# A fused linear-attention and gated-FFN kernel: the first k block turned as fp32, and one new order for all operations

## The chip, the cores and the metric

The kernel runs on one core of a Trainium2 chip. The core has five engines with a queue each: TensorE (PE: matmuls, with weight loads shown as PEld), VectorE (DVE), ScalarE (ACT), GpSimd (POOL) and SyncE (SP, which here only issues DMAs). Each takes its instructions in program order and waits on semaphores for what the others make. The metric is the device time of one execution in microseconds (us); lower is better.

## What is computed

Attention with exponential feature maps over q, k and v of shape [8, 8, 576, 64] (batch, head, token, head dimension), then a feed-forward block with a gate over the 4608 tokens of width 512:

```python
def phi(x):
    proj = np.einsum('bhsd,df->bhsf', x, w_phi)             # w_phi: 64 x 128
    proj = proj - np.max(np.abs(proj), axis=-1, keepdims=True)
    return np.concatenate([np.exp(proj), np.exp(-proj)], axis=-1)
q_p, k_p = phi(q), phi(k)
kv  = np.einsum('bhsf,bhsd->bhfd', k_p, v)
z   = np.sum(k_p, axis=2)
num = np.einsum('bhsf,bhfd->bhsd', q_p, kv)
den = np.einsum('bhsf,bhf->bhs', q_p, z)[..., None] + 1e-06
x   = (num / den).transpose(0, 2, 1, 3).reshape(4608, 512)
gate = np.maximum(x @ w_gate, 0.0)                          # w_gate, w_val: 512 x 1536
out  = gate * (x @ w_val) @ w_out                           # w_out: 1536 x 512
```

## The kernel before

All matmuls are bf16 with fp32 accumulation in eight PSUM banks. A batch is 512 tokens in four chunks of 128 (`C` = 4) and 64 left over; the left-over tokens of pairs of batches make a ninth group. The heads are taken in three groups, 0 to 1, 2 to 4 and 5 to 7 (`HEADS`).

The order of everything is written out by hand as data: `ORDER` is a string of some 2,000 words, one for each operation, such as `ke.0.1.2.0:4@kp0`. The name before the first dot picks the function `do_ke`, the numbers are its arguments, the digits behind the colon are its PSUM banks, and what stands behind `@` is the buffer that a tile takes in its ring. The last lines of the kernel run through the words and call the functions, so that each engine's queue is the words of that engine in the order of the string. A word that comes later in the string can still run earlier in time if it is on another engine and waits for nothing.

The words that the texts below speak of, for batch `b`, head group `j`, chunk `i`:

- Loads. `lf` (L445, SP) brings k of batch 0, heads 2 to 4, as fp32 into the storage of `xTm`; `lk` (POOL) brings other k with a cast to bf16, `lm` and `lq` small pieces of k and q in the same way, `lv` and `lw` bring v, `wl` a third of w_val (0) or w_gate (1), `wo` a third of w_out, `ln` the left-over q. `wr` (L393, on ACT's queue) and `wq` (the same on SP's) load w_phi twice over into 128 partitions, `wd` (L402) casts it, `w1` and `wa` make the second layout of it.
- First k. `cf` and `cg` (L453) cast what `lf` brought, on DVE and ACT. `k0` (L584) turns six blocks of 128 x 128 on PE as bf16 matmuls with the identity, `k1` (L587) copies the result to `kT`, `k2` (L605) multiplies with w_phi: twelve matmuls into four banks, one for each chunk. Later batches turn k on DVE (`kt`, `ku`) and multiply in `kr`.
- Features of k. `ke` (L614, ACT) is the exponential of plus or minus the projection, `kx` (L622, DVE) the largest absolute value, `kk` and `kp` (L631, L642, ACT) its exponential. `vs`, `vq`, `vo` (POOL) and `vd`, `vp` (DVE) scale v by it. `kv` (L718, PE) sums over the tokens, `kc` (L729, ACT) copies the sums.
- Features of q. `q0` and `q1` turn q, `qb` (L764, PE) projects it, `qe` (L793, ACT) and `qx` (L801, DVE) as for k; `qy`, `qz`, `qu` and `qw` spread the largest value over the partitions (`qy` on PE at L811 with an fp32 identity, `qz` the DVE maximum `my` at L819).
- Division. `nu` (L841, PE) multiplies q's features with the sums, `nt`, `nv` and `nr` (L862, L872, L880, DVE) add the two signs and invert, `nx` (L884, POOL) normalizes to `xu`.
- Feed-forward. Batch 0 turns `xu` on PE (`xp` at L906, copied by `xa` on ACT), then works by chunk: `pv` and `pg` (L1029), 16 matmuls of 128 columns each. Otherwise `fv` and `fg` (L1000) make value and gate with four matmuls of 512 columns, `ga` (L1021) multiplies them, `fo` (L1061) is the second matmul, `od` stores.
- `zz.n` (L425) is n matmuls of 256 columns of zeros into a bank that nobody reads: filler for PE.

Batch 0's attention has to be through its first chunk before the feed-forward can start; from then on feed-forward matmuls of one batch are mixed with the attention of the next.

Of the kernel before, what the change touches and what calls it, by code (L numbers as in the profile page):

```python
# [8 lines left out]
FP32 = mybir.dt.float32  # L9
# [7 lines left out]
ms.0 ms.4@vr0 wr ms.3@vr1 lf id sl ms.5 ms.6 ms.2 lw.0.1 lw.0.0 if cf.1 lk.0.2 lk.0.0 wd cg.0  # L17
zz.18:0 k0.1:0 k1.1:0@kT0 lm.0.1 lm.0.0 zz.1:1 w1:2 lq.0.1 lq.0.0 wa:2 zz.2:1 k2.1:0345
ke.0.1.2.0:4@kp0 lv.0.2 kx.0.1.1:3@mk0 lv.0.1 ke.0.1.3.1:5 kx.0.1.2:4 zz.2:1 k0.2:2 k1.2:2@kT1
ke.0.1.1.0:3 ke.0.1.2.1:4 kx.0.1.0:0 kx.0.1.3:5 ke.0.1.1.1:3 zz.7:1 k2.2:2674 ke.0.2.0.1:2@kp1  # L20
ke.0.2.2.0:7 kx.0.2.1:6@mk1 ke.0.2.0.0:2 ke.0.1.0.0:0 k0.0:3 k1.0:3@kT1 wl.0.0 ke.0.1.3.0:5
kx.0.2.2:7 kx.0.2.0:2 lv.0.0 zz.6:1 q0.1:3 q1.1:3@qT0 ke.0.2.1.1:6 ke.0.2.2.1:7 kx.0.2.3:4 zz.1:1
q0.0:5 q1.0:5@qT1 ke.0.2.1.0:6 zz.4:1 k2.0:2736 lm.1.1 lk.1.3 lm.1.0 kx.0.0.0:2@mk2 ke.0.1.0.1:0
kx.0.0.2:3 ke.0.2.3.0:4 kx.0.0.1:7 kp.0.2.1:4 kk.0.1.0@ek0 lq.1.2 kk.0.1.1 qb.1.0:0 qe.0.1.0.1:0@qp0
vo.1@vs0 kp.0.2.0:4 kx.0.0.3:6 vp.2:4@vs1 vs.0.1.0 qb.1.1:5 qe.0.1.1.0:5@qp1 qe.0.1.0.0:0 qx.0.1.1:5
ke.0.0.1.0:7@kp2 qx.0.1.0:0 vd.0.2.0:4 vs.0.1.1 kk.0.0.0@ek1 ke.0.0.3.0:6 zz.18:1 qb.0.1:0
ke.0.0.2.1:3 ke.0.0.1.1:7 qx.0.0.1:0 qb.0.2:7 qx.0.0.2:7 ke.0.2.3.1:4 wl.0.1 kk.0.0.1 vq.0.1
ke.0.0.0.1:2 ke.0.0.3.1:6 ke.0.0.0.0:2 zz.6:1 qb.0.0:6 vs.0.0.0@vs2 vq.0.0 qx.0.0.0:6 zz.5:1
# [232 lines left out]
def kernel(  # L261
# [16 lines left out]
    P = 128  # L278
# [615 lines left out]
    def do_ny(bk, b, i):  # L894
        normalize(nc.vector, b, i)
# [257 lines left out]
```

## Time and profile before

| | |
|---|---|
| time, median of 3 runs | 376.44 us (373.83, 376.44, 376.68) |
| profiled execution | 377.31 us, of which the span from first to last instruction is 375.5 us |
| mean granted PE clock over the span | 0.990 |
| bytes read from and written to HBM | 37.81 MB and 9.44 MB |
| matmuls in the span | 3614, 75 of them fillers |

A line of the timeline has the start, the time from the first start to the last end of the instructions that it merges, the engine, the line in the code, the operation, the tiles written and read and their count; brackets tell how long the engine stood idle before it and what ended that. A line of the stages has the stage, its length, and the busy time of PE, weight loads, DVE, ACT and POOL with their counts, then the PE clock that was granted (1.00 is full), the mean number of DMA queues busy as a share, and GB/s. A DMA line has the transfer, its count, its size and the time from issue to landing.

### The profile page before, as it was taken

The numbers are of one execution on the slowest core, as the hardware profiler recorded it, in microseconds if no ns is written. First come the engines' busy times: TensorE is split into PE (matmuls) and PEld (weight loads), VectorE is DVE, ScalarE is ACT, GpSimd is POOL, SyncE is SP. The second block draws the span as 40 slices with busy tenths as digits, with TensorE's granted clock in tenths as the row PEclk, the third lists the DMA queues.
The fourth block names the chain that finished last, engine by engine and source line by source line (L and its number), as shares of the span: only waits on it lengthen the run. The fifth ranks groups of instructions, "written<-read, shape, count | busy, mean of one in ns | idle before, by whom it ended". The sixth has DMA issues, their size and how long they took to land.

```text
span 375.5 us, 9202 instructions
## 1 busy us (share of the span) xinstructions
PE 367.3 (98%) x3614; PEld 196.7 (52%) x3614; DVE 290.4 (77%) x672; ACT 228.5 (61%) x550; POOL 157.3 (42%) x163
## 2 busy tenths in 40 slices
PE   8798999999999999999999999999999999999996
PEld 5567857446544554564455444554444644444444
DVE  5969999998989899999978795888675646534441
ACT  4979996999768873987865556846764301212111
POOL 8774496549349138912770343513045013100000
PEclk9969999999999999999999999999999999999999
DMA  9999998973974992393438052183330022200114
GB/s 141 248 201 199 149 133 119 151 117 58 176 184 71 181 139 70 68 190 76 100 61 152 17 95 66 46 148 51 107 89 17 2 72 82 58 2 15 41 30 141
DMA packets 90381, 38.10 MB, mean 101 GB/s; under 512 B 64226, under 2 KB 85602, under 8 KB 90338
## 3 DMA queue, kind: packets, MB, share of 16 engines
q0 software_dynamic: 33504, 15.03, 31.4%
q1 hardware_dynamic: 56560, 22.29, 26.7%
q8 instruction: 28, 0.46, 0.5%
q10 hardware_dynamic: 274, 0.20, 0.2%
q14 instruction: 15, 0.12, 0.1%
HBM read 37.81 MB, written 9.44 MB: 126 GB/s over the span
## 4 chain that ended last, share of the span: by engine, by line
PE 93%; DVE 2%; DMA 2%; POOL 1%; ACT 1%; issue 0%; POOLq 0%; ACTq 0%
PE bank L1000 47%; PE bank L1061 24%; PE bank L718 6%; PE bank L841 4%; PE bank L1029 4%; PE bank L778 2%; PE bank L562 2%; DMA qn<-in_q_dram 2%; PE bank L982 1%; PE bank L1092 1%; PE bank L764 0%; PE bank L425 0%; POOL kn L434 0%; DVE mk L622 0%; DVE u L872 0%
## 5 line engine op out<-in xcount | busy, mean ns | idle before, releaser
L1061 PE MATMUL bank<-wo,h 128*128 128x512 bf16 x420 | 97.8, 379 | 0.0
L614 ACT ACTIVATE kp<-bank 128x384 bf16<-128x384 f32 x192 | 83.5, 509 | 16.4 <-PE bank L562 11.2
L1015 ACT CAST val<-bank 128x512 bf16<-128x512 f32 x81 | 47.2, 594 | 73.1 <-PE bank L1000 67.5
L1021 DVE SCALAR_TENSOR_TENSOR h<-bank,val 128x512 bf16<-128x512 f32 x100 | 67.1, 681 | 28.9 <-PE bank L1000 14.4
L1000 PE MATMUL bank<-xTs,wv 128*128 128x512 bf16 x352 | 87.1, 379 | 0.0
L1000 PE MATMUL bank<-xTs,wg 128*128 128x512 bf16 x352 | 86.4, 379 | 0.0
L884 POOL TENSOR_TENSOR xu<-u,r 128x512 bf16<-128x512 f32 x36 | 37.2, 1040 | 99.2 <-DVE r L880 72.5
L793 ACT ACTIVATE qp<-bank 128x512 bf16<-128x512 f32 x128 | 70.0, 619 | 10.7 <-PE bank L778 9.0
L1061 PEld LDWEIGHTS <-h 128*128 128x128 bf16 x420 | 39.2, 98 | 45.8 <-issue 2.4
L669 POOL TENSOR_TENSOR vs<-vn,ek 128x780 bf16<-128x780 f32 (+3 forms) x40 | 52.8, 1341 | 24.0 <-ACT ek L631 13.4
L1000 PEld LDWEIGHTS <-wg 128*128 128x128 bf16 x400 | 37.5, 98 | 41.6 <-issue 1.1
L1000 PEld LDWEIGHTS <-wv 128*128 128x128 bf16 x400 | 37.0, 98 | 41.1 <-issue 1.3
L622 DVE TENSOR_REDUCE mk<-bank 128x3 f32<-128x384 f32 x96 | 49.7, 541 | 3.5 <-ACT kp L614 1.4
L801 DVE TRANSPOSE_TENSOR_REDUCE maxq<-bank 128x16 f32<-128x512 f32 x64 | 42.4, 693 | 7.1 <-ACT qp L793 3.2
L872 DVE TENSOR_TENSOR u<-bank,t 128x195 f32<-128x195 f32 (+1 forms) x108 | 33.8, 331 | 2.4 <-POOL xu L884 0.4
L862 DVE TENSOR_TENSOR t<-bank,cq 128x195 f32<-128x195 f32 (+1 forms) x96 | 29.9, 327 | 7.0 <-PE bank L841 6.2
L841 PEld LDWEIGHTS <-qp 128*128 128x128 bf16 x512 | 22.5, 98 | 11.9 <-issue 1.5
L697 POOL TENSOR_TENSOR vr<-vm,ek 64x520 bf16<-64x520 f32 x16 | 16.9, 1055 | 23.4 <-ACT ek L631 15.9
L841 PE MATMUL bank<-kv,qp 128*128 128x65 bf16 x512 | 25.3, 193 | 0.0
L718 PEld LDWEIGHTS <-kp 128*128 128x128 bf16 x640 | 23.0, 101 | 3.9 <-ACT qp L793 1.0
L718 PE MATMUL bank<-vs,kp 128*128 128x65 bf16 x512 | 23.8, 198 | 0.0
L1070 ACT COPY ob<-bank 128x512 f32<-128x512 f32 x19 | 11.3, 595 | 20.4 <-PE bank L1061 19.5
(97 smaller groups left out, 355.2 us busy)
## 6 DMA issues: line engine op xcount, KB each, us to landing
out_dram<-ob SPq DMA_DIRECT2D x31, 256.0 KB, 2.4
vn<-in_v_dram SPq DMA_DIRECT2D x24, 256.0 KB, 4.2
kn<-in_k_dram POOLq DMA_DIRECT2D x7, 512.0 KB, 9.7
qn<-in_q_dram POOLq DMA_DIRECT2D x7, 512.0 KB, 7.6
wv<-in_moe_w_val_dram POOLq DMA_DIRECT2D x3, 512.0 KB, 11.4
wg<-in_moe_w_gate_dram POOLq DMA_DIRECT2D x3, 512.0 KB, 8.6
wo<-in_moe_w_out_dram POOLq DMA_DIRECT2D x3, 512.0 KB, 7.7
out_dram<-ob SPq DMA_DIRECT2D x9, 128.0 KB, 2.3
```

The source lines that it names most:

```text
L614: nc.scalar.activation(kp_of(3 * b + j)[:, i, s].rearrange("p n f -> p (n f)"), bank[bk[0]][:, 0 : 3 * F], AF.Exp, scale=(1.0, -1.0)[s],)
L622: nc.vector.tensor_reduce(mk_of(3 * b + j)[:, :, i], bank[bk[0]][:, 0 : 3 * F].rearrange("p (n f) -> p n f", f=F), axis=AX.X, op=ALU.max, ...
L669: nc.gpsimd.tensor_tensor(vs_of(3 * b + j)[:, s, 0:n].rearrange("p n i e -> p (n i) e")[:, :, 0:e], src[:, lo:hi].rearrange("p h i e -> p ...
L718: nc.tensor.matmul(out_ps[:, h - lo, s, :], lhsT=lhsT, rhs=rhs, start=(at == 0), stop=(at == 2 * n * (C + 1) - 1),)
L793: nc.scalar.activation(qp_of(4 * b + i)[:, s, 4 * hq : 4 * hq + 4].rearrange("p h m -> p (h m)"), bank[bk[0]], AF.Exp, scale=(1.0, -1.0)[s],)
L801: nc.vector.tensor_reduce(maxq[:, :, i, 4 * hq : 4 * hq + 4].rearrange("p t h -> p h t"), bank[bk[0]].rearrange("p (h t u) -> p h t u", h= ...
L841: nc.tensor.matmul(bank[bk[0]][:, E * n : E * (n + 1)], lhsT=qp_of(4 * b + i)[:, s, h, :], rhs=kv_of(b)[:, h, s, 0:E],)
L884: eng.tensor_tensor(xu_of(n).rearrange("p (h d) -> p h d", d=D), u_of(n)[:, :, 0:D], r_of(n).to_broadcast([P, H, D]), op=ALU.mult,)
L1000: nc.tensor.matmul(bank[bk[0]], lhsT=w[:, dc, P * f : P * f + P], rhs=xT(g)[:, dc, :], start=(dc == 0), stop=(dc == NDC - 1),)
L1015: nc.scalar.copy(val_of(NFC * g + f), bank[bk[0]])
L1021: nc.vector.scalar_tensor_tensor(h2_of(g, f), bank[bk[0]], 0.0, val_of(NFC * g + f), op0=ALU.max, op1=ALU.mult)
L1061: nc.tensor.matmul(bank[bk[0]], lhsT=h2_of(g, f)[:, P * t : P * t + P], rhs=wo_sb[:, f, :], start=(f == 0), stop=(f == NFC - 1),)
```

## The change

The order string is replaced as a whole. The words are the same but for these: `wr`, `cf.1`, `cg.0`, `k0.1`, `k1.1`, `k2.0`, `k2.1` and `k2.2` are gone; `wq`, `kf.1`, `kf.0`, `kg.1`, `kh.0` and `k3.j.c` (six of them) are new; and the fillers are 77, placed otherwise. `lf`'s fp32 data is no longer cast: `kf.c` turns it on PE as fp32 with the fp32 identity, three matmuls for each half, and `kg.1` (DVE) and `kh.0` (ACT) copy the two halves to `kT` as bf16. `k3` is `k2` cut in two, two banks each. w_phi is issued by SP behind `lf` instead of by ACT. The last 1,469 words keep their order; banks and buffers are assigned anew everywhere.

Up to the first turned x block the order before was:

```
ms.0 ms.4@vr0 wr ms.3@vr1 lf id sl ms.5 ms.6 ms.2 lw.0.1 lw.0.0 if cf.1 lk.0.2 lk.0.0 wd cg.0
zz.18:0 k0.1:0 k1.1:0@kT0 lm.0.1 lm.0.0 zz.1:1 w1:2 lq.0.1 lq.0.0 wa:2 zz.2:1 k2.1:0345
ke.0.1.2.0:4@kp0 lv.0.2 kx.0.1.1:3@mk0 lv.0.1 ke.0.1.3.1:5 kx.0.1.2:4 zz.2:1 k0.2:2 k1.2:2@kT1
ke.0.1.1.0:3 ke.0.1.2.1:4 kx.0.1.0:0 kx.0.1.3:5 ke.0.1.1.1:3 zz.7:1 k2.2:2674 ke.0.2.0.1:2@kp1
ke.0.2.2.0:7 kx.0.2.1:6@mk1 ke.0.2.0.0:2 ke.0.1.0.0:0 k0.0:3 k1.0:3@kT1 wl.0.0 ke.0.1.3.0:5
kx.0.2.2:7 kx.0.2.0:2 lv.0.0 zz.6:1 q0.1:3 q1.1:3@qT0 ke.0.2.1.1:6 ke.0.2.2.1:7 kx.0.2.3:4 zz.1:1
q0.0:5 q1.0:5@qT1 ke.0.2.1.0:6 zz.4:1 k2.0:2736 lm.1.1 lk.1.3 lm.1.0 kx.0.0.0:2@mk2 ke.0.1.0.1:0
kx.0.0.2:3 ke.0.2.3.0:4 kx.0.0.1:7 kp.0.2.1:4 kk.0.1.0@ek0 lq.1.2 kk.0.1.1 qb.1.0:0 qe.0.1.0.1:0@qp0
vo.1@vs0 kp.0.2.0:4 kx.0.0.3:6 vp.2:4@vs1 vs.0.1.0 qb.1.1:5 qe.0.1.1.0:5@qp1 qe.0.1.0.0:0 qx.0.1.1:5
ke.0.0.1.0:7@kp2 qx.0.1.0:0 vd.0.2.0:4 vs.0.1.1 kk.0.0.0@ek1 ke.0.0.3.0:6 zz.18:1 qb.0.1:0
ke.0.0.2.1:3 ke.0.0.1.1:7 qx.0.0.1:0 qb.0.2:7 qx.0.0.2:7 ke.0.2.3.1:4 wl.0.1 kk.0.0.1 vq.0.1
ke.0.0.0.1:2 ke.0.0.3.1:6 ke.0.0.0.0:2 zz.6:1 qb.0.0:6 vs.0.0.0@vs2 vq.0.0 qx.0.0.0:6 zz.5:1
qy.0.0:2 vs.0.0.1 ke.0.0.2.0:3 vd.0.2.1:4 qz.0.0:2@my0 qe.0.0.1.1:0 qb.1.2:3 qx.0.1.2:3 zz.2:1
qb.1.3:4 qe.0.1.1.1:5 lw.1.0 qe.0.0.2.1:7@qp2 qx.0.1.3:4 qe.0.0.0.0:6 qe.0.0.1.0:0 qb.0.3:2
qx.0.0.3:2 vo.0 qe.0.0.2.0:7 kv.0.1:5 kt.1.1@kT1 lv.1.2 qe.0.0.0.1:6 kv.0.2:0 kc.0.1:5@kv0 qy.0.2:5
qu.0.0@mz0 qy.0.1:6 kt.1.0@kT2 wl.1.0 qe.0.0.3.1:2@qp3 qz.0.1:6@my0 kv.0.0:7 kc.0.2:0 lw.1.1
qu.0.1@mz1 qz.0.2:5@my1 qy.0.3:0 qu.0.2@mz2 nu.0.0.2:6 lv.1.3 qz.0.3:0@my0 qe.0.0.3.0:2 nu.0.0.1:1
qw.0.0@cq0 nt.0.0.2:6@t0 wl.1.1 nt.0.0.1:1@t1 nv.0.0.2:6@u0 lv.1.1 kc.0.0:7 nu.0.0.0:7 nt.0.0.0:7@t2
wl.0.2 nv.0.0.1:1 nv.0.0.0:7 qe.0.1.2.1:3 nr.0.0@r0 qe.0.1.3.1:4 lv.1.0 qw.0.1 ln.0.1 zz.3:0
kr.1.1:0526 kx.1.1.0:0@mk2 qe.0.1.2.0:3 nu.0.1.1:1 nt.0.1.1:1@t2 ke.1.1.1.0:5@kp2 nu.0.1.2:7
qe.0.1.3.0:4 nu.0.1.0:3 nt.0.1.0:3@t1 ke.1.1.0.1:0 nt.0.1.2:7@t0 nv.0.1.1:1@u1 nv.0.1.0:3 nv.0.1.2:7
nr.0.1@r1 nx.0.0@xu0 xp.0.0:4
```

and it is now:

```
ms.0 id lm.0.1 ms.2 lk.0.2 ms.3@vr0 ms.5 lk.0.0 if sl ms.6 lf ms.4@vr1 wq wd lm.0.0 zz.12:7 kf.1:0
lv.0.1 kg.1:0@kT0 kf.0:1 kh.0:1 k3.1.1:23 w1:4 ke.0.1.2.0:2@kp0 kx.0.1.3:3@mk0 zz.1:7 k3.1.0:56
kx.0.1.0:5 zz.5:7 k0.2:0 ke.0.1.2.1:2 ke.0.1.3.0:3 kx.0.1.1:6 kx.0.1.2:2 wa:4 lq.0.0 ke.0.1.0.1:5
ke.0.1.0.0:5 zz.3:7 k0.0:1 lq.0.1 lm.1.1 kk.0.1.0@ek0 ke.0.1.1.1:6 k1.2:0@kT1 k1.0:1@kT2 k3.2.0:42
lm.1.0 ke.0.1.3.1:3 kx.0.2.0:4@mk1 k3.2.1:50 kx.0.2.3:0 kx.0.2.2:5 ke.0.2.1.1:2@kp1 kk.0.1.1
ke.0.2.1.0:2 ke.0.1.1.0:6 lv.0.2 kx.0.2.1:2 lw.0.1 ke.0.2.3.0:0 zz.2:7 k3.0.1:13 kx.0.0.2:1@mk2
lv.0.0 zz.12:7 k3.0.0:62 ke.0.2.0.0:4 ke.0.2.0.1:4 kx.0.0.3:3 zz.3:7 q0.0:4 kp.0.2.1:0 ke.0.2.2.0:5
ke.0.2.2.1:5 kp.0.2.0:0 kx.0.0.0:6 ke.0.0.3.0:3@kp2 lk.1.3 ke.0.0.0.0:6 zz.2:7 q0.1:5 kx.0.0.1:2
kk.0.0.0@ek1 q1.0:4@qT0 ku.1@kT3 ke.0.0.2.1:1 kk.0.0.1 zz.2:7 qb.0.0:4 wl.0.0 q1.1:5@qT1 qx.0.0.0:4
vp.2:0@vs0 ke.0.0.0.1:6 zz.4:7 qb.1.0:5 ke.0.0.3.1:3 ke.0.0.2.0:1 qb.0.1:6 ke.0.0.1.0:2 qx.0.0.1:6
qb.0.2:3 ke.0.0.1.1:2 vo.1@vs1 vd.0.2.0:0 vs.0.1.1 zz.1:7 qb.1.1:1 qe.0.0.0.1:4@qp0 qe.0.0.1.1:6@qp1
qe.0.0.1.0:6 vs.0.1.0 qx.0.1.1:1 qx.0.1.0:5 qe.0.1.1.0:1 qe.0.1.1.1:1 zz.4:7 qb.1.2:2 qx.0.0.2:3
zz.17:7 qy.0.0:6 lq.1.2 vo.0@vs2 wl.0.1 vd.0.2.1:0 vs.0.0.1 lw.0.0 qe.0.0.0.0:4 qz.0.0:6@my0
qb.0.3:1 qx.0.1.2:2 vq.0.1 qe.0.1.0.1:5 zz.1:7 qb.1.3:4 vq.0.0 zz.1:7 kv.0.1:6 ke.0.2.3.1:0
qx.0.1.3:4 qe.0.1.0.0:5 qu.0.0@mz0 qx.0.0.3:1 kv.0.2:0 kt.1.1@kT1 qe.0.0.2.0:3@qp2 kc.0.1:6@kv0
qy.0.1:5 nu.0.0.1:6 qe.0.0.2.1:3 qw.0.0@cq0 kc.0.2:0 nt.0.0.1:6@t0 qe.0.1.3.0:4@qp3 vs.0.0.0
kv.0.0:3 lw.1.0 qz.0.1:5@my1 kc.0.0:3 qe.0.1.2.1:2 nu.0.0.2:0 nv.0.0.1:6@u0 qy.0.3:5 qu.0.1@mz1
nt.0.0.2:0@t1 zz.1:7 nu.0.1.0:6 qw.0.1 nu.0.0.0:3 qz.0.3:5@my2 nv.0.0.2:0 zz.1:7 nu.0.1.2:5
nt.0.0.0:3@t2 nu.0.1.1:0 qe.0.1.2.0:2 qe.0.1.3.1:4 nt.0.1.0:6@t3 nv.0.0.0:3 qy.0.2:2 nv.0.1.0:6@u1
nr.0.0@r0 qe.0.0.3.1:1 lv.1.0 qz.0.2:2@my0 lv.1.2 lv.1.3 wl.1.0 nt.0.1.2:5@t0 nx.0.0@xu0 zz.4:7
kr.1.1:3642 qe.0.0.3.0:1 nt.0.1.1:0@t1 zz.1:7 nu.0.2.1:1 xp.0.0:7
```

Behind that point `wl.0.2`, the last third of w_val, stands in POOL's queue behind `nx.0.0` to `nx.0.3`, `ln.0.1` and `ln.0.0`; before, it stood ahead of all of them. Fifteen groups `pv` and `pg` now precede the first `fv`, where twelve did.

```diff
-    mk_of = ring("mk", 3, [P, 3, 4], FP32)
-    ek_of = ring("ek", 3, [P, 2, 3, 4], FP32)
-    vs_of = ring("vs", 3, [P, 2, 3, 4, EP], BF16)
+    mk_of = ring("mk", 6, [P, 3, 4], FP32)
+    ek_of = ring("ek", 6, [P, 2, 3, 4], FP32)
+    vs_of = ring("vs", 4, [P, 2, 3, 4, EP], BF16)
...
-    qp_of = ring("qp", 4, [P, 2, 8, P], BF16)
+    qp_of = ring("qp", 5, [P, 2, 8, P], BF16)
...
+    def do_kf(bk, cp):
+        for n in range(3):
+            nc.tensor.matmul(
+                bank[bk[0]][:, P * n : P * n + P],
+                lhsT=k_first()[:, n, P * cp : P * cp + P],
+                rhs=identf,
+                is_transpose=True,
+            )
+
+    def turn_first(copy, bk, cp):
+        dst = kT_of(1).rearrange("p n m a -> p (n m a)").rearrange("p (n c m) -> p n c m", c=2, m=P)
+        copy(dst[:, :, cp, :], bank[bk[0]][:, 0 : 3 * P].rearrange("p (n m) -> p n m", m=P))
+
+    def do_kg(bk, cp):
+        turn_first(nc.vector.tensor_copy, bk, cp)
+
+    def do_kh(bk, cp):
+        turn_first(nc.scalar.copy, bk, cp)
+
+    def do_k3(bk, j, cp):
+        T = kT_of(j).rearrange("p n m a -> p (n m a)").rearrange("p (k m) -> p k m", m=P)
+        heads = [1, 2, 0] if j == 0 else [0, 1, 2]
+        for k_, n in enumerate(heads):
+            for e in range(2):
+                r = slice(D * e, D * (e + 1))
+                nc.tensor.matmul(
+                    bank[bk[e]][:, F * n : F * (n + 1)],
+                    lhsT=T[r, 2 * k_ + cp, :],
+                    rhs=w64[r, :],
+                    start=(k_ == 0),
+                    stop=(k_ == 2),
+                )
```

`do_vd` and `do_vp` now also take the head group of two, which no word uses; three further new functions (`do_vz`, `do_nh`, `do_ni`) are not called by any word either.

More of the change, by code (lines that the diff above doesn't have):

```diff
@@ L23 @@
[L23 to L28, printed above, removed]
```

487 lines of the change are left out of this document (249 added, 238 removed).

## The prediction

> **What bounds the kernel now.** I read the page first (engine shares, granted clock by slice), then the busy time in stages, then the first 35 us instruction by instruction.
>
> ```profile
> span 375.5 us, 9202 instructions
> PE 367.3 (98%) x3614; PEld 196.7 (52%) x3614; DVE 290.4 (77%) x672; ACT 228.5 (61%) x550; POOL 157.3 (42%) x163
> PEclk9969999999999999999999999999999999999999
> 60.00:100.00 40.00, 39.94 (x523) 21.46 (x521) 38.39 (x100) 33.95 (x85) 21.57 (x22) 1.00 0.89 119
> 200.00:300.00 100.00, 99.99 (x909) 49.83 (x909) 75.97 (x170) 58.12 (x137) 31.71 (x28) 1.00 0.32 68
> ```
>
> TensorE (PE) is busy 98% of the span, and in the stages from 60 us on it has no idle time: columns are the stage, its length, then busy time of PE, weight loads, VectorE (DVE), ScalarE (ACT) and GpSimd (POOL), the clock, DMA. The change removes nothing of that work, so it can only win in the head, before PE is fed without gaps. The slice at 0.6 of the clock lies in that head. Cut into stretches of 3.4 us, the columns as above:
>
> ```profile
> 9.68:13.10 3.42, 2.38 (x28) 1.62 (x25) 3.19 (x7) 3.42 (x10) 1.85 (x4) 1.00 1.13 304
> 16.50:19.92 3.42, 2.15 (x13) 1.08 (x13) 2.74 (x5) 2.79 (x9) 2.67 (x4) 0.99 1.47 188
> 19.92:23.33 3.41, 3.40 (x18) 1.04 (x17) 2.92 (x6) 3.41 (x7) 3.41 (x5) 0.50 1.36 203
> 23.33:26.74 3.41, 3.41 (x61) 3.35 (x59) 1.83 (x4) 1.32 (x4) 2.44 (x4) 0.51 1.17 207
> ```
>
> PE was busy 2.15 of 3.42 us, and for the next 6.8 us its clock is halved; with 2.38 busy the clock had stayed up. At half clock PE becomes the late one: DVE falls to 1.83 busy, ACT to 1.32. Elsewhere in the head DVE and ACT are the full ones. What the DVE waits for there, and when the first normalized token block reaches PE:
>
> ```profile
> 19.61 0.72 DVE L801 TRANSPOSE_TENSOR_REDUCE maxq<-bank 128x16 f32<-128x512 f32 x1 [0.68 <-PE bank L764]
> 22.89 3.32 PEld L718 LDWEIGHTS <-kp 128*128 128x128 bf16 x60 [0.84 <-ACT qp L793]
> 26.93 0.29 DVE L819 TENSOR_REDUCE my<-bank 128x32 f32<-128x128 f32 x1 [1.77 <-ACT kv L729]
> 30.94 0.40 PE L906 MATMUL bank<-ident,xu 128*128 128x128 bf16 x4 [0.90 <-POOL xu L884]
> ```
>
> The two bracketed DVE waits, 0.68 and 1.77 us, are its dearest after its first maximum: 2.45 us. The larger one stands behind the 60 weight loads of kv, which took 3.32 us at half clock.
>
> **The change, part by part.** First, the start of the chain.
>
> ```profile
> 0.73 0.46 SPq L445 DMA_DIRECT2D xTm<-in_k_dram  x1
> 0.74 1.14 ACTq L393 DMA_DIRECT2D w64f<-in_w_phi_dram  x1
> 1.06 4.02 PE L425 MATMUL bank<-zero 128*128 128x256 bf16 x18 [1.06 <-DVE zero L412]
> 4.05 0.43 DVE L453 CAST kn<-xTm 128x256 bf16<-128x256 f32 x1 [0.91 <-DMA xTm<-in_k_dram]
> 4.87 0.85 PE L584 MATMUL bank<-ident,kn 128*128 128x128 bf16 x6
> 5.64 0.28 DVE L402 CAST w<-w64f 128x128 bf16<-128x128 f32 x1 [1.16 <-DMA w64f<-in_w_phi_dram]
> 5.79 0.55 DVE L587 COPY kT<-bank 128x768 bf16<-128x768 bf16 x1
> 6.59 0.51 PE L605 MATMUL bank<-w,kT 64*128 64x128 bf16 x12
> 7.08 1.13 DVE L622 TENSOR_REDUCE mk<-bank 128x3 f32<-128x384 f32 x2 [0.75 <-PE bank L605]
> 7.75 0.93 PE L425 MATMUL bank<-zero 128*128 128x256 bf16 x7
> 13.60 1.95 DVE L622 TENSOR_REDUCE mk<-bank 128x3 f32<-128x384 f32 x4
> 20.47 0.45 PE L811 MATMUL bank<-identf,maxq 128*128 128x128 f32 x1
> ```
> ```profile
> xTm<-in_k_dram SPq DMA_DIRECT2D x1, 384.0 KB, 3.3
> w64f<-in_w_phi_dram ACTq DMA_DIRECT2D x1, 64.0 KB
> ```
>
> Now: k lands at 4.05, both casts, six transposes, then the copy, which stands behind the cast of w_phi, and that waits for its DMA until 5.64; six more steps end in the first maximum at 7.08. With the change, k still lands at 4.05, since it stays first on SP. The casts go (0.43 on DVE, a longer one on ACT). Three fp32 transposes follow at once; the 18 fillers at 4.02/18 = 0.22 us each against 0.93/7 = 0.13 later show that PE still runs slow here. The profile has no such transposes back to back. They cost between 0.73 (one fp32 at 0.45 and two at the bf16 pace, 0.85/6 = 0.14) and 1.35 (three at 0.45); I take 0.9, nearer the low end since issues overlap: 4.95. w_phi, 64 KB behind 384 KB on one queue, lands between 4.05 (with k) and 6.15 (its old landing plus the 0.5 us that SP spends on k's issue). I take 4.6, k's 3.3 us times 64/384 behind k; its cast ends at 4.9, under cover of the transposes. The new DVE copy lies between 0.43 and 0.55: 0.5, so 5.45. Six matmuls, half of the 0.51 and doubled for the slow clock, end at 5.95. First maximum at 6.0: **1.1 us earlier**; by the bounds from 1.3 earlier to 0.3 later (w_phi at 6.15, then 0.28, 0.5 and 0.5). The second half, through ACT's copy, runs beside it, since ACT lost its longer cast.
>
> The fp32 transposes replace as many bf16 ones; at most 6 x (0.45 - 0.14) = 1.9 us of PE time, in a stretch that 12 instead of 18 opening fillers leave empty. On PE the 77 fillers (75 before) cost 2 x 0.13 = 0.3 us, in gaps.
>
> Second, what POOL issues.
>
> ```profile
> 1.43 1.68 POOL L434 DMA_DIRECT2D kn<-in_k_dram  x2
> 3.10 1.26 POOL L473 DMA_DIRECT2D km<-in_k_dram  x2
> 7.40 0.34 PEld L584 LDWEIGHTS <-kn 128*128 128x128 bf16 x6 [0.26 <-DMA kn<-in_k_dram]
> 12.12 0.62 PE L746 MATMUL bank<-ident,qn 128*128 128x128 bf16 x8 [0.57 <-DMA qn<-in_q_dram]
> ```
>
> One small k issue (1.26/2 = 0.63 us) now goes ahead of the k of heads 5 to 7, which landed just before 7.40: now 8.0. DVE has done its first four maxima by 6.0 + 1.95 = 7.95; transposes (0.4) put the next copy at 8.4, a **new wait of 0.5 us**. PE stands with k0.0 and the k3 steps behind it. q goes behind a v load: some 0.8 us later than the 12.12 above, but in the new order DVE has all twelve maxima of k (5.9 us of them) and ACT 23 of 24 exponentials ahead of it; I leave 0.3 us for it. New waits: 0.8.
>
> Third, fillers and order. Where the clock fell (2.15 busy), the changed order has 4, 17, 1 and 1 fillers between the q projections, the maximum's transpose and kv: 23 x 0.13 = 3 us in one such stretch. If the clock stays up, the 60 loads at 3.32 us halve, and the kv steps end before DVE has drained its q maxima; kv's copy then no longer holds DVE, and both waits (2.45) go. The deeper buffers (mk and ek 6, vs 4, qp 5) only loosen waits and cost nothing; what hides their effect is that DVE itself is late next.
>
> On the clock the Trainium skill differs. "TensorE: Matmul & The Clock Gate", section "HAM oscillation — how this bites in real kernels", says that the clock falls after PE has stood idle for more than about 3.4 us. The trace disagrees: it fell after a stretch with 2.15 us of work in it. By the page no fall would come in either kernel, so that the second rival below would be nil.
>
> The sum on the DVE: 1.1 (start) + 2.45 (waits) - 0.8 (new waits) = 2.75, say **2.7 us**. I carry it to the end: up to 100 us DVE (38.39 of 40) and PE (39.94) are both full, so PE can use a lead only if DVE has it too, and beyond that PE alone counts. The profiled execution took 377.31 (375.5 span and 1.8 around it), 0.9 above the median 376.44: it would be 374.6, and the median **373.7**.
>
> **Rivals.** (1) Better: PE's wait of 0.90 for the first x block goes too and no new wait comes: 1.1 + 2.45 + 0.9 = 4.4 us, 372.0. For it: both queues move alike; against: DVE is full. (2) The clock falls all the same, in another stretch. Between the wait for k (8.0) and that for q, and between q's two halves, PE has thin stretches near the 2.15 to 2.38 that decide; then 17 fillers in a row stand ahead of the maximum's transpose at double cost. The two DVE waits stay; 1.1 - 0.8 = 0.3 gained: 376.1. (3) Slower: a weight piece comes late.
>
> ```profile
> 37.82 1.04 POOL L884 TENSOR_TENSOR xu<-u,r 128x512 bf16<-128x512 f32 x1 [1.28 <-DVE r L880]
> 39.55 0.71 POOL L484 DMA_DIRECT2D qm<-in_q_dram  x1
> 34.59 1.06 PE L1029 MATMUL bank<-xTs,wv 128*128 128x128 bf16 x16
> 46.10 1.90 PE L1000 MATMUL bank<-xTs,wv 128*128 128x512 bf16 x8
> wo<-in_moe_w_out_dram POOLq DMA_DIRECT2D x1, 512.0 KB, 6.7
> wg<-in_moe_w_gate_dram POOLq DMA_DIRECT2D x1, 512.0 KB, 9.4
> wv<-in_moe_w_val_dram POOLq DMA_DIRECT2D x1, 512.0 KB, 13.6
> ```
>
> The last third of w_val (wl.0.2) moves on POOL behind all four normalizations of batch 0 and both qm loads: 37.82 + 1.04 - 2.7 + 2 x 0.71 = 37.6. Its first user is the first 512-wide group, at 46.10 now; three more 16-matmul groups (0.9 each without the drain) stand ahead of it, and the lead takes 2.7 off: due at about 46.1, so 8.5 us after issue. Loads of this size took 6.7, 9.4 and 13.6; the last had two others in front, which this one has not. At 9.4 PE waits 0.9; at 13.6 it waits 5.1: 378.8, slower than before from 11.2 us upward. (4) w_phi comes no earlier: start 0.3 later, 2.45 - 0.3 - 0.8 = 1.35, 375.1; this is also the case that the change doesn't do what it says. (5) The transposes do not keep the clock up, so that the slow start lasts one stretch more.
>
> ```profile
> 9.68:13.10 3.42, 1.47 (x11) 0.80 (x9) 0.00 (x0) 1.00 1.13 304
> 16.50:19.92 3.42, 1.25 (x10) 0.89 (x11) 0.00 (x0) 0.99 1.47 188
> ```
>
> These are the fillers alone (PE, loads, DVE). Eight fillers (1.1), twelve matmuls (0.51) and twelve transposes (0.85) would take 2.5 us more, some 1.0 of it inside the wait for k: 1.5 lost, 375.2. Against it: of the 2.38 us in the stretch that kept its clock only 1.47 were fillers and nearly all the rest transposes, less than the 2.15 that lost it. The same page, in "Part 4: PE-mode transpose", says that transposes do not count as PE activity in the same way; by that the first stretch should have lost the clock, and the trace disagrees.
>
> **How the numbers follow.** Forecast 50% (373.7; its own range 372.2 to 375.4 by the start's bounds and waits of 0 to 1.5 in place of 0.8), rival 1 11%, 2 20%, 3 13%, 4 4%, 5 2%. 1% (3.8 us) is about what can be told from no change: below 372.7 is faster, above 380.2 slower. Faster: most of rival 1 and a quarter of the forecast, 22%. Slower: the part of rival 3 in which the clock falls too, and the same for wo further on, 8%. Same: 70%. Range 371.6 to 378.2: it leaves out the edge of rival 1, the upper half of rival 3 and its pairings.
>
> **What would show it.** First maximum near 6.0, not 7.08; a wait for kn near 8; granted clock at 1.00 from 16 to 30 us; no wait of 1.77 ahead of my; first x transposes near 28 in place of 30.94, and no PE wait at the first 512-wide group. A clock of 0.50 anywhere after 7 us, PE waiting for wv near 46, or w_phi landing after 5.6 proves it wrong.

## The result, and the profile after

The changed kernel takes 372.12 us in the median of 18 runs (371.99 to 373.92). The kernel before, run beside it, takes 374.64 (18 runs, 373.82 to 377.02). The ratio is 0.9932, its 95% interval 0.9916 to 0.9948: 2.5 us less, where 2.7 were forecast. That the two sizes agree is largely luck: most of the terms behind the forecast were not right. Two more sets of the unaltered changed kernel (a_same and a_same2 below) gained 0.9 and 1.7 us.

The page of the changed kernel (span and matmul count; busy time of the engines; the granted clock in 40 slices):

```profile
span 369.9 us, 9208 instructions
PE 362.8 (98%) x3616; PEld 194.9 (53%) x3616; DVE 288.1 (78%) x671; ACT 226.6 (61%) x550; POOL 157.4 (43%) x163
PEclk9999999999999999999999999999999999999999
```

The half-clock slice is gone, and PE's busy time is 4.5 us smaller. Now the start, from its timeline:

```profile
0.73 0.45 SPq L446 DMA_DIRECT2D xTm<-in_k_dram  x1
1.25 0.73 SPq L391 DMA_DIRECT2D w64f<-in_w_phi_dram  x1
1.06 2.74 PE L426 MATMUL bank<-zero 128*128 128x256 bf16 x12 [1.06 <-DVE zero L413]
4.26 1.03 PE L616 MATMUL bank<-identf,xTm 128*128 128x128 f32 x6 [0.46 <-DMA xTm<-in_k_dram]
5.32 0.48 ACT L625 CAST kT<-bank 128x384 bf16<-128x384 f32 x1 [3.31 <-PE bank L616]
5.89 0.23 DVE L403 CAST w<-w64f 128x128 bf16<-128x128 f32 x1 [3.12 <-DMA w64f<-in_w_phi_dram]
6.03 0.55 DVE L625 CAST kT<-bank 128x384 bf16<-128x384 f32 x1
6.64 0.34 PE L639 MATMUL bank<-w,kT 64*128 64x128 bf16 x6 [1.35 <-DVE kT L625]
7.05 2.05 DVE L667 TENSOR_REDUCE mk<-bank 128x3 f32<-128x384 f32 x4 [0.47 <-PE bank L639]
8.07 0.50 PE L585 MATMUL bank<-ident,kn 128*128 128x128 bf16 x6
```

The fp32 turn of k is done by 5.3 us, but DVE's copy of it stands behind the cast of w_phi, and w_phi is there only at 5.89, later than the 5.64 of before. The first maximum starts at 7.05; it was 7.08. The transposes of the later k need no wait at 8.07. What DVE waited for in the first 40 us (total, times, longest):

```profile
DVE w L403 <- DMA w64f<-in_w_phi_dram: 3.1, 1, 3.1
DVE zero L413 <- PEq L1199: 0.8, 1, 0.8
DVE mk L667 <- PE bank L639: 0.5, 1, 0.5
```

Nothing after the first maximum. And what PE waited for in the whole span:

```profile
PE bank L639 <- DVE kT L625: 1.4, 1, 1.4
...
PE bank L1091 <- ACT xTs L982: 0.4, 1, 0.4
...
PE bank L811 <- DVE qT L801: 0.2, 1, 0.2
```

Neither answer has the 0.68, 1.77 or 0.90 that the prediction quoted (the lines left out are two waits before the first maximum and one of 0.4 for a later kT), and PE never waits for a weight piece. The stages of 3.4 us (PE, loads, DVE, ACT, POOL, clock, DMA share, GB/s):

```profile
4.70:8.10 3.40, 2.05 (x27) 1.43 (x26) 1.74 (x5) 1.56 (x4) 3.40 (x6) 1.00 1.34 231
16.50:19.92 3.42, 3.42 (x25) 2.20 (x24) 3.42 (x6) 3.42 (x8) 3.24 (x4) 1.00 1.30 201
19.92:23.33 3.41, 3.41 (x91) 3.03 (x91) 3.36 (x9) 3.35 (x9) 1.78 (x3) 1.00 1.36 203
60.00:100.00 40.00, 40.00 (x456) 20.34 (x453) 38.12 (x88) 34.56 (x87) 20.89 (x21) 1.00 0.89 131
```

Where PE had 2.15 us of work it now has 3.42, and the clock stays up. The landmarks further on, from the timeline:

```profile
20.48 1.97 PEld L765 LDWEIGHTS <-kp 128*128 128x128 bf16 x60
23.28 0.28 DVE L866 TENSOR_REDUCE my<-bank 128x32 f32<-128x128 f32 x1
26.74 0.40 PE L968 MATMUL bank<-ident,xu 128*128 128x128 bf16 x4
44.37 1.03 PE L1062 MATMUL bank<-xTs,wv 128*128 128x512 bf16 x4
```

The 60 loads of kv take 1.97 us in place of 3.32, the first x block comes at 26.74 in place of 30.94 (4.2 us earlier), and the first 512-wide group at 44.37 waits for nothing.

**Where the two traces part.** Each kernel has the same 3,539 matmuls besides the fillers. Counting them back from the last, one can ask of every kernel when it had as many still to come. The table (worked out from the traces' matmul records) gives that time for b_fill, the kernel before with twelve fillers more, whose clock never falls, and for the others how much later (+) or earlier (−) they were, in us. From 2,571 to go (79 us) the matmuls come in the same order in all.

| matmuls still to come | 3450 | 3050 | 2500 | 1500 | 1000 | 0 |
|---|---|---|---|---|---|---|
| b_fill, at | 21.5 | 42.0 | 86.5 | 175.8 | 232.4 | 368.6 |
| before | +1.82 | +3.27 | +3.46 | +3.47 | +3.47 | +3.47 |
| b_kf | +0.08 | +0.09 | +0.36 | +0.35 | +0.62 | +0.62 |
| after | −0.65 | −1.18 | −1.31 | −1.55 | −2.03 | −2.16 |
| a_same (after, run again) | +0.57 | +0.05 | −0.09 | −0.31 | −0.79 | −0.92 |
| a_rings | +0.28 | −0.23 | −0.38 | −0.59 | −1.07 | −1.19 |

So the 5.6 us between the two profiled executions (375.5 − 369.9) are three things: 3.47 between an execution with the clock fall and one without, nearly all of it lost by 42 us (b_kf, the old order without a fall, agrees with b_fill there to 0.1); 1.18 in the head; and 0.98 behind 42 us, most of it where both kernels run the same operations in the same order and both show PE full. The second is missing in a_same. The third is in all ten profiled executions of the changed order (0.49 to 1.00) and in none of the four of the old order (0.00 to 0.53 the other way). Outside the span 0.4 us of it is given back: the changed kernel's time is 2.2 us above its span (372.08 − 369.9), the old one's 1.8.

### The profile page after: what moved, and what is told of

It is laid out like the page before. It is cut to its first block, busy times and chain, and to the rows that moved or that the text cites. A ratio compares the mean times of both kernels' runs of the same rounds, so it can differ in the third digit from the quotient of the medians.

```text
span 369.9 us, 9208 instructions
## 1 busy us (share of the span) xinstructions
PE 362.8 (98%) x3616; PEld 194.9 (53%) x3616; DVE 288.1 (78%) x671; ACT 226.6 (61%) x550; POOL 157.4 (43%) x163
## 4 chain that ended last, share of the span: by engine, by line
PE 94%; DVE 2%; ACT 2%; DMA 1%; issue 0%; SPq 0%; ACTq 0%
PE bank L1062 47%; PE bank L1123 25%; PE bank L765 5%; PE bank L888 4%; PE bank L1091 4%; PE bank L825 2%; PE bank L563 2%; DMA w64f<-in_w_phi_dram 1%; DVE mk L667 1%; PE bank L426 1%; ACT qp L840 1%; PE bank L1154 1%; PE bank L1044 1%; PE bank L811 1%; PE bank L858 0%
## 5 line engine op out<-in xcount | busy, mean ns | idle before, releaser
L659 ACT ACTIVATE kp<-bank 128x384 bf16<-128x384 f32 x192 | 84.4, 522 | 17.3 <-PE bank L563 12.1
L840 ACT ACTIVATE qp<-bank 128x512 bf16<-128x512 f32 x128 | 69.1, 625 | 10.3 <-PE bank L825 9.0
L1135 DVE COPY ob<-bank 128x512 f32<-128x512 f32 x16 | 10.9, 684 | 16.1 <-PE bank L1123 13.8
L765 PEld LDWEIGHTS <-kp 128*128 128x128 bf16 x640 | 21.7, 97 | 2.7 <-ACT qp L840 0.2
```

Source lines behind the costliest of these rows:

```text
L659: nc.scalar.activation(kp_of(3 * b + j)[:, i, s].rearrange("p n f -> p (n f)"), bank[bk[0]][:, 0 : 3 * F], AF.Exp, scale=(1.0, -1.0)[s],)
L765: nc.tensor.matmul(out_ps[:, h - lo, s, :], lhsT=lhsT, rhs=rhs, start=(at == 0), stop=(at == 2 * n * (C + 1) - 1),)
L840: nc.scalar.activation(qp_of(4 * b + i)[:, s, 4 * hq : 4 * hq + 4].rearrange("p h m -> p (h m)"), bank[bk[0]], AF.Exp, scale=(1.0, -1.0)[s],)
```

## The experiments

All times stand beside the kernel before on the same chip. The three sets of it had medians of 374.27 (33 runs), 375.39 (29) and 375.03 (28).

**a_same**: the changed kernel as it is.

> The changed kernel again, unaltered, as the yardstick for the runs beside it: 372.1 us, in some executions 1 us more; granted clock 1.00 from 7 us to the last matmul where it is 372.1.

373.35 us (10 runs, 372.04 to 374.06), ratio 0.9965 (0.9949 to 0.9981). Its timeline:

```profile
4.42 1.51 PE L616 MATMUL bank<-identf,xTm 128*128 128x128 f32 x6 [0.63 <-DMA xTm<-in_k_dram]
7.30 0.56 DVE L667 TENSOR_REDUCE mk<-bank 128x3 f32<-128x384 f32 x1 [0.63 <-PE bank L639]
27.96 0.40 PE L968 MATMUL bank<-ident,xu 128*128 128x128 bf16 x4
```

The same six transposes take 1.51 us, not 1.03: PE runs at half rate until 10.08 us by the trace's clock records, where the first profile had the rise at 4.66. The first x block comes 1.22 us later, and the time is 1.23 us longer (373.31 against 372.08). These two times fit the two levels in the 18 runs of the result, 11 at 371.99 to 372.24 and 7 at 373.05 to 373.92.

**a_k0**: the fp32 turn undone; first k is cast to bf16 again.

```diff
-... lf ms.4@vr1 wq wd lm.0.0 zz.12:7 kf.1:0 lv.0.1 kg.1:0@kT0 kf.0:1 kh.0:1 k3.1.1:23
+... lf ms.4@vr1 wq cf.1 cg.0 wd lm.0.0 zz.12:7 k0.1:0 lv.0.1 k1.1:0@kT0 k3.1.1:23
```

> The changed kernel with the first k cast and turned as bf16 again, w_phi still on SP. If w_phi's landing (5.89 us in the profile of the changed kernel) sets the start, as its profile suggests, the fp32 path is worth nothing here: first DVE maximum within 0.15 us of 7.05 and the time within 0.3 us of the unaltered one. If the fp32 path itself brought the gain that was forecast, it is 0.5 to 1.1 us slower.

373.8 us (12 runs), ratio 0.9983 (0.9970 to 0.9996), 0.45 above a_same and so between the two expectations: a few tenths for the fp32 turn are not excluded.

```profile
6.03 0.23 DVE L403 CAST w<-w64f 128x128 bf16<-128x128 f32 x1 [1.54 <-DMA w64f<-in_w_phi_dram]
7.18 0.56 DVE L667 TENSOR_REDUCE mk<-bank 128x3 f32<-128x384 f32 x1 [0.47 <-PE bank L639]
```

The old path reaches the first maximum at 7.18, between the 7.05 and 7.30 of the new one: both end up waiting for w_phi at 6.0. Without the fp32 turn DVE stands idle 1.54 us for it, with it 3.12.

**a_wfirst**: w_phi ahead of k on SP.

```diff
-... sl ms.6 lf ms.4@vr1 wq wd lm.0.0
+... sl ms.6 wq lf ms.4@vr1 wd lm.0.0
```

> The changed kernel with w_phi issued on SP ahead of k instead of behind it. If w_phi sets the start: it lands near 3.5 to 4.5 us, k some 0.4 us later than 4.2, the first DVE maximum comes near 6.3 instead of 7.05, and 0.4 to 0.8 us of that reach the end. If the start is covered by later waits (k of heads 5 to 7 and q have to land), the first maximum moves and the time doesn't: within 0.2 us.

374.76 us (12 runs), ratio 1.0003 (0.9988 to 1.0019): no gain is left. No theory had that.

```profile
0.74 0.74 SPq L391 DMA_DIRECT2D w64f<-in_w_phi_dram  x1
5.37 0.56 DVE L403 CAST w<-w64f 128x128 bf16<-128x128 f32 x1 [2.60 <-DMA w64f<-in_w_phi_dram]
6.52 1.51 PE L616 MATMUL bank<-identf,xTm 128*128 128x128 f32 x6 [2.72 <-DMA xTm<-in_k_dram]
```

First in the queue, w_phi is cast only 0.5 us earlier: 4.6 us behind its issue, as long as when it stood behind k (1.25 to 5.89). And k, issued 0.8 us later (1.55 in place of 0.73), is there 2.3 us later, so that the first maximum moves back, to 8.61. The clock rises only at 11.98 here, which the time includes. Little of w_phi's delay is k ahead of it on SP.

**a_nozz**: 65 of the 77 fillers left out; only the opening twelve stay.

> The changed kernel without 65 of its 77 fillers; only the 12 at the very start stay, so that what is computed is unchanged. If the fillers keep the clock up: the granted clock falls to 0.50 for one or more stretches of 3.4 us between 7 and 30 us and the time rises by 1.5 to 4 us. If the gain is the order's alone and fillers are mere load: no fall, time the same or up to 0.5 us lower.

374.18 us (10 runs), ratio 0.9985 (0.9969 to 1.0001), 0.83 above a_same. The stages and one row:

```profile
14.50:17.90 3.40, 2.44 (x6) 0.41 (x5) 3.40 (x7) 3.40 (x10) 3.02 (x5) 0.50 1.36 202
21.30:24.80 3.50, 3.50 (x66) 3.44 (x64) 1.83 (x4) 1.97 (x6) 0.39 (x1) 0.51 1.27 216
```
```profile
25.01 0.36 DVE L907 TENSOR_TENSOR t<-bank,cq 128x195 f32<-128x195 f32 x1 [1.88 <-PE bank L886]
```

The clock is at half from 7.65 to 24.72 us and DVE waits 1.88 us for PE at the end, the same picture as in before. So without fillers the clock falls. What the fall costs is not shown here: the six runs with a mean clock of 0.982 or less have a median of 374.2, the four at 1.00 one of 374.1. As the clock reads full until its first rise, those four may have run at half rate for long too; no trace of them was kept. That a fall of 17 us costs less here than one of 6.8 us in before would fit a price paid only where PE is late, in the kv steps, but no run tests it.

**b_again** and **b_fill**: the kernel before, run again, and with twelve fillers more where its clock fell.

```diff
-ke.0.0.3.0:6 zz.18:1 qb.0.1:0
+ke.0.0.3.0:6 zz.24:1 qb.0.1:0
...
-ke.0.0.0.0:2 zz.6:1 qb.0.0:6
+ke.0.0.0.0:2 zz.12:1 qb.0.0:6
```

> The kernel before, unaltered, profiled again. If its spread (373.8 to 377.0 us) is the clock: a time near 374.5 goes with a shorter half-clock stretch, or one at another place, than the 6.8 us of the first profile. If the spread has another source, the half-clock stretch is the same at every time.

> The kernel before with 12 fillers more, 6 in each of its two PE gaps between 16 and 19.2 us; nothing else changed. If the lost clock is most of the gain: no half-clock stretch after 7 us, the waits of 0.68 and 1.77 us ahead of DVE gone or small, and 1.5 to 2.5 us less than before (372 to 373). If the order makes the gain: within 0.7 us of before.

b_again gave one run, 377.22 us, with the same fall from 19.81 to 26.64 us, so it didn't show what an execution without the fall looks like. b_fill did: 374.44 us (12 runs, 373.80 to 375.36) against 375.39, ratio 0.9977 (0.9959 to 0.9995), and no execution with a fall. The 0.95 lies between the two expectations: between medians the fall is neither most of the gain nor nothing. Its stages, then its timeline:

```profile
13.40:16.80 3.40, 3.21 (x27) 2.43 (x26) 3.40 (x8) 3.29 (x11) 3.22 (x4) 1.00 1.28 231
16.80:20.20 3.40, 3.15 (x21) 1.82 (x20) 2.72 (x5) 3.06 (x9) 2.87 (x4) 1.00 1.48 189
```
```profile
18.95 0.72 DVE L801 TRANSPOSE_TENSOR_REDUCE maxq<-bank 128x16 f32<-128x512 f32 x1 [0.68 <-PE bank L764]
23.66 0.29 DVE L819 TENSOR_REDUCE my<-bank 128x32 f32<-128x128 f32 x1
27.67 0.40 PE L906 MATMUL bank<-ident,xu 128*128 128x128 bf16 x4 [0.90 <-POOL xu L884]
```

The 1.77 wait is gone, the 0.68 and the 0.90 stay, and the first x block is 3.27 us earlier than in before. Fillers alone thus undo the fall. Its price is 3.4 us between the profiled executions (377.22 − 373.83), but the latter is one of b_fill's fastest. And the fall doesn't always happen: of the 90 runs of before beside the experiments, 26 show a mean clock of 0.995 or less, at 375.4 us and up, with a median of 376.7; the other 64 take 373.8 to 376.1, with a median of 374.5. That puts the price at 2.2 us; at 2.4 for the 18 of the 26 that, like the first profile, have a mean clock near 0.990. In none of the three sets is the median a run with the fall.

**b_kf**: the kernel before with only the fp32 turn of the first k; w_phi stays on ACT.

```diff
-... if cf.1 lk.0.2 lk.0.0 wd cg.0 zz.18:0 k0.1:0 k1.1:0@kT0 lm.0.1 ... zz.2:1 k2.1:0345
+... if lk.0.2 lk.0.0 wd zz.18:0 kf.1:0 kg.1:0@kT0 kf.0:2 kh.0:2 lm.0.1 ... zz.2:1 k3.1.1:45 k3.1.0:03
```

> The kernel before with one part of the change alone: the first k turned as fp32 and its projection in two halves, w_phi still on ACT's queue, the rest of the order and all fillers as before. If w_phi's landing at 5.64 us sets the start: first DVE maximum within 0.3 us of 7.08 and the time within 0.5 us of before. If the casts set it, as the forecast had it: near 6.0 and about 1 us less.

375.47 us (12 runs), ratio 1.0014 (0.9989 to 1.0039): nothing. Of the 12 runs 5 have the fall; the other 7 have a median of 375.0, against 374.7 for the runs of before in this set without it.

```profile
5.67 0.26 DVE L402 CAST w<-w64f 128x128 bf16<-128x128 f32 x1 [2.52 <-DMA w64f<-in_w_phi_dram]
7.17 1.02 DVE L666 TENSOR_REDUCE mk<-bank 128x3 f32<-128x384 f32 x2 [0.81 <-PE bank L638]
```

DVE again waits for w_phi, to 5.67, and the first maximum starts at 7.17. The new path shortens a branch that isn't the last.

**a_wr**: w_phi issued by ACT, as before, in the changed kernel.

```diff
-ms.0 id lm.0.1 ... lf ms.4@vr1 wq wd lm.0.0
+ms.0 wr id lm.0.1 ... lf ms.4@vr1 wd lm.0.0
```

> The changed kernel with w_phi on ACT's queue, where it was before the change. If the queue behind k delays it: it lands near 5.6 instead of 5.89, first maximum 0.2 to 0.3 us earlier, time equal or 0.3 us less. If SP's queue is the better place: 0.3 us or more slower.

373.8 us (10 runs), ratio 0.9953 (0.9928 to 0.9978) against that set's 375.39.

```profile
5.85 0.23 DVE L403 CAST w<-w64f 128x128 bf16<-128x128 f32 x1 [3.08 <-DMA w64f<-in_w_phi_dram]
```

5.85 from ACT, where it is issued at 0.74, and 5.89 from SP behind k, where it is issued at 1.25: the place in the queues makes no difference.

**a_same2, a_warm, a_rings, a_vmpool**, side by side: the changed kernel again; with six fillers more ahead of the first k steps; with the old buffer counts; and with the first two v-memory loads moved from SP to a later place on POOL, in case their packets hold w_phi up.

```diff
-zz.12:7 kf.1:0 lv.0.1 kg.1:0@kT0 kf.0:1 kh.0:1 k3.1.1:23
+zz.14:7 kf.1:0 lv.0.1 kg.1:0@kT0 kf.0:1 kh.0:1 zz.4:7 k3.1.1:23
```
```diff
-mk 6, ek 6, vs 4, qp 5
+mk 3, ek 3, vs 3, qp 4
```
```diff
-lq.0.1 lm.1.1 ... kx.0.2.1:2 lw.0.1 ke.0.2.3.0:0 ... vs.0.0.1 lw.0.0 qe.0.0.0.0:4
+lq.0.1 lw.0.1 lw.0.0 lm.1.1 ... kx.0.2.1:2 ke.0.2.3.0:0 ... vs.0.0.1 qe.0.0.0.0:4
```

> The changed kernel unaltered beside the next three: two groups of times, near 372.1 where the clock rises to full before 5 us and near 373.3 where it rises only near 10 us.

> The changed kernel with 6 fillers more in two places where PE waits at the start: 14 instead of 12 ahead of the first k, and 4 between its transposes and its projection. If the late rise of the clock makes the slower group: the clock is full by 7 us in the profile, and the slower group goes or shrinks, median 372.0 to 372.4. If the groups have another source: same mix, or 0.3 us slower by the fillers.

> The changed kernel with the buffer counts of before: mk and ek 3, vs 3, qp 4, in the changed order. If deeper buffers cost and bring nothing while DVE is late, as the prediction had it: within 0.3 us of the unaltered one. If the new order needs them: 0.5 us or more slower, with DVE or ACT waiting for mk, ek, vs or qp before 35 us.

> The changed kernel with the two loads of v's left-over tokens moved from SP, right behind w_phi, to POOL behind q. If their small packets, between w_phi's on the same DMA engines, are what brings w_phi in as late as 5.9 us: it lands at 5.0 or earlier, the first DVE maximum comes 0.5 us or more before 7.05, the time falls by 0.3 to 0.8 us. If the POOL loads or the queue's own latency hold it: within 0.2 us of 5.9, time equal, or slower by POOL's two further issues.

| | median us (runs) | ratio to before (375.03) |
|---|---|---|
| a_same2 | 373.34 (12) | 0.9950 (0.9927 to 0.9973) |
| a_warm | 372.66 (6) | 0.9926 (0.9898 to 0.9953) |
| a_rings | 372.60 (12) | 0.9924 (0.9900 to 0.9948) |
| a_vmpool | 373.45 (12) | 0.9950 (0.9930 to 0.9970) |

a_warm has its clock rise at 3.71 us and no run above 372.83, its median a little above the 372.0 to 372.4 expected. In its timeline the first x block is back near the 26.74 of the first profile:

```profile
26.89 0.40 PE L968 MATMUL bank<-ident,xu 128*128 128x128 bf16 x4
```

It is the steadiest version measured, 0.7 us below a_same2 beside it, though with overlapping intervals and only six runs; its lowest run (372.08) is no lower than the changed kernel's (371.77). The deeper buffers bring nothing: a_rings isn't slower, and its 0.74 below a_same2 is within the overlap of the intervals. Moving the v-memory loads leaves w_phi's cast at 5.90, so their packets aren't what delays it.

**The tail**, where the table has 0.98 us. One of the places, in the timeline of b_fill:

```profile
211.99 0.58 ACT L1015 CAST val<-bank 128x512 bf16<-128x512 f32 x1 [3.33 <-DVE h L1021]
212.24 0.10 PEld L1000 LDWEIGHTS <-wg 128*128 128x128 bf16 x1
212.63 1.02 PE L1000 MATMUL bank<-xTs,wg 128*128 128x512 bf16 x4
212.63 0.74 PEld L1000 LDWEIGHTS <-wg 128*128 128x128 bf16 x4 [0.29 <-issue]
```

and the same operations in the changed kernel:

```profile
210.00 0.58 ACT L1077 CAST val<-bank 128x512 bf16<-128x512 f32 x1 [3.12 <-PE bank L1062]
210.41 1.18 PEld L1062 LDWEIGHTS <-wg 128*128 128x128 bf16 x6
210.62 1.24 PE L1062 MATMUL bank<-xTs,wg 128*128 128x512 bf16 x5
```

In the old kernel the cast that empties a bank waits for DVE, and the weight loads of the next group break off for 0.29 us until just after that cast ends (211.99 + 0.58 = 212.57); in the new one the cast waits for PE alone, and the loads run through. There are six such places of 0.07 to 0.18 us between 122 and 212 us, at the same operations in after, a_same, a_wr and a_rings. Between these kernels and b_fill the order from 79 us on is the same; 1,022 of the 1,167 words there that name a bank name another one, and buffers are numbered anew. a_rings rules out the buffer counts. At the place shown the words tell what differs:

```
before: vb.4.0:1@val1 ... ga.4.0:6@hs6 ... fv.4.5:0 ... va.4.5:0@val1 ... fg.4.5:0
now:    vb.4.0:6@val2 ... ga.4.0:7@hs8 ... fv.4.5:5 ... va.4.5:5@val1 ... fg.4.5:7
```

The late cast is `va.4.5`. In the old order it writes `val1`, which `ga.4.0` reads on DVE until 211.90 (211.21 + 0.69); in the new one that value lies in `val2`. And the next group, `fg.4.5`, goes into bank 0, which this cast has to empty; in the new order it takes another one. So here the buffers given out and the banks given out work together. For the other five places, and for what either would do by itself, that is argued, not shown: neither was exchanged alone.

## Why the prediction was right, and where its steps failed

**The number** came out right in good part by luck. The prediction took 2.7 off 376.44 and said 373.7; the time is 372.12. The difference of 2.5 us holds because the kernel before, too, was lower in its 18 runs (374.64) than in the three that the prediction had; by the 90 runs, 376.44 is a time that only executions with the clock fall have. Of the 2.5, the clock's part between medians is under 1 us (b_fill's 0.95), where the sum has 2.45. The rest came from the order in the head and from the tail. The forecast's own range is also added up wrongly: with the start from 1.3 earlier to 0.3 later and waits of 0 to 1.5 it goes from 372.7 to 375.8, not from 372.2 to 375.4, and 372.12 lies below both. The time is that of rival 1 (372.0), and PE's wait of 0.90 and both DVE waits are gone as it had them, but not its 1.1 us at the start.

**"It can only win in the head"** failed. PE's busy time doesn't tell a matmul stream that runs through from one that pauses between weight loads: before reads 39.94 of 40 us there and after 40.00, and still 0.98 of the 2.16 us that separate after from b_fill came behind 42 us. The words of the tail keep their order, but not their banks and buffers, and the prediction has no term for that.

**The start (1.1 us)** failed: 0.03 us. The step that failed is the landing of w_phi, estimated at 4.6 by scaling k's 3.3 us with the size; its cast began at 5.89, near the late one of the prediction's bounds (4.05 to 6.15) and past the 5.6 that the prediction named as a sign against it. At the start the size doesn't scale the time (the last section has the rows). Rival 4 had this mechanism with a 4% chance. a_wfirst and a_wr moved its issue and a_vmpool the loads behind it, and its cast never started before 5.37. The transposes were sized about right: six in 1.51 us at half rate is 0.75 for three, where 0.9 was taken.

**New waits (0.8 us)** failed too: none. With the start not earlier, DVE reaches the second k when it did before, and kn is there (8.07); for q PE waits 0.2 us (for DVE's copy of the turned q) and DVE not at all. The two errors, 1.1 too much and 0.8 too little, nearly cancel.

**Clock and waits (2.45 us)**: the mechanism was right, shown by b_fill; a_nozz shows from the other side that without the fillers the clock falls. The size, where the fall happens, is 2.2 to 2.4 us between medians and 3.4 between the profiled executions, where the first x block comes later by the whole of it; that the first agrees with 2.45 doesn't confirm the two DVE waits as its account, since b_fill keeps the 0.68. How often was missed: the one profiled execution was of the 26 in 90 that have the fall. What the changed order gains beyond that is the 0.68 wait, PE's 0.90 (rival 1's part), and the tail: 373.83 (b_fill) to 372.08 from profile to profile; in ratios to before, 0.9977 against 0.9932, 0.9965 and 0.9950, which is 0.5 to 1.7 us.

**The rivals.** Rival 3 was far off: the last third of w_val is issued at 35.18, takes 6.0 us and is used at 44.37 without a wait. Rival 2 was right that a fall can come elsewhere: a_k0, a_rings and a_vmpool had one stretch at half clock near 7.3 to 10.7 us, and so, by their mean clock of 0.995, had 7 of the 40 runs of the unaltered changed kernel; but PE isn't late there, and those runs lie at 373.2 to 373.4, in the upper level and not above it. Rival 5 (2%) was right in its outcome: in a_same and a_same2 the slow start lasts longer, to 10.08 and 9.97 us, and a_same is 1.2 us slower by it, where rival 5 said 1.5. Its cause isn't needed for that: in a_wfirst the stretch from 1.74 to 5.15 us has 2.06 us of fillers and no transpose, and the clock didn't rise behind it; in after it stays up through the one from 4.66 to 8.07, which has transposes.

**What the sum has no term for** is the rise of the clock. With it at 10.08 in place of 4.66 us the changed kernel gains nothing in the head over b_fill (+0.05 against −1.18 at 3,050 to go). The change itself seems to have made this likelier: twelve opening fillers in place of eighteen, and a PE that waits 1.4 us for w_phi. In the four profiled executions of the old order the rise came at 3.7 to 6.2 us, in the ten of the changed order at 3.7 to 4.7 in six and at 10.0 to 12.0 in four; a_warm's six fillers more give 3.71 and leave one level in six runs. The Trainium skill, "TensorE: Matmul & The Clock Gate", section "What's actually happening", says that activity is judged in windows of 3413 ns that run freely and don't start with the kernel. The runs agree: the falls lasted 6.83 us in before (two windows), 3.41 in a_k0, 17.07 in a_nozz (five), and one and the same kernel rose at 4.66, 10.08 and 9.97. The prediction weighed another section of that page and treated the clock as a function of the work alone.

Left open: how much work in a window is enough. The prediction saw the border between 2.15 and 2.38 us; counted back from the rises and falls in whole windows, 2.06 of 3.41 us kept the clock in after (4.66 to 8.07) and 1.93 in a_warm (3.71 to 7.12), while 2.07 lost it in before (16.43 to 19.84), so the sum in the window just ahead doesn't decide alone. Also open are why w_phi's packets are slow; which banks and buffers matter in the tail; and the 1 to 2 us by which runs of before without a fall differ among themselves.

## What to carry to other kernels

Before costing a step that the profile shows as dear, look whether the profiled execution is the typical one: here its largest wait belonged to a fall that a bit over a quarter of the runs have. Shortening a branch at the start pays only up to the next arrival, so give that arrival the range of its nearest rows, and ask what the sum is at the late end. Where PE reads as full, compare two kernels by the time at which equal work is left, since small pauses between weight loads count as busy.

## What the runs showed of the hardware

At the start the size of a load says little of its landing. From the changed kernel's DMA answer for the first 3 us (transfer, queue, count, size of one, median us from issue to landing):

```profile
xTm<-in_k_dram SPq DMA_DIRECT2D x1, 384.0 KB, 3.4
kn<-in_k_dram POOLq DMA_DIRECT2D x1, 192.0 KB, 5.5
vm<-in_v_dram SPq DMA_DIRECT2D x2, 64.0 KB, 4.5
km<-in_k_dram POOLq DMA_DIRECT2D x1, 32.0 KB, 4.2
```

The largest load, issued first, is the quickest. Those behind it took 4.2 to 5.5 us whatever their size and queue, and w_phi, issued at 1.25 and cast at 5.89, 4.6. To be first isn't enough: in a_wfirst w_phi was first, issued at 0.74, and was cast at 5.37, 4.6 us later again, while k as the second took 4.8. The packets in the traces say where the time goes. k's 384 packets of 1 KB are under way from 1.85 to 3.66 us in after, before w_phi's 128 of 512 B, from 3.55 to 5.50; in a_wfirst the two overlap, w_phi's from 2.24 to 4.64 and k's from 2.63 to 5.83, so that k takes 3.2 us in place of 1.8. w_phi's packets take 1.7 to 2.4 us in all fourteen profiled executions. That the loads share the DMA engines' time fits this; why a load of 64 KB takes so long wasn't tested.

The granted clock reads 1.00 in the first stretches, while matmuls run at half rate: 0.22 us for a filler, and 1.51 against 1.03 us for six fp32 transposes. Until the first rise the column isn't evidence.
